# Decode kernel: shared weight loads in folds and PV, PV's blocks picked and p summed on VectorE

## The chip, the core and the metric

The kernel runs on one core of one Trainium2 chip. The metric is device time in microseconds of one execution; three executions of the kernel before took 203.09, 203.16 and 203.21 us (median 203.16). A core has a matrix engine (TensorE, PE in the profile; its weight loads are the rows PEld), VectorE (DVE), ScalarE (ACT), GpSimd (POOL) and SyncE (SP), which here only issues DMAs. SBUF is the working memory with 128 partitions; PSUM is where TensorE writes, in 8 banks of 512 fp32 a partition.

## What is computed

One token passes an attention block and a gated MLP, each with a layer norm in front and a residual behind. Everything is bf16 outside of sums. There are 32 heads of 128, a cache of 4096 positions for each, and a model width of 640.

```
q = (layernorm(x) @ wq)                          # 640 -> 32 heads x 128
scores = einsum("bhqd,bhkd->bhqk", q, k) * 128 ** -0.5
p = softmax(scores)                              # over 4096 positions
o = einsum("bhqk,bhkd->bhqd", p, v)
h = x + o.reshape(1, 1, 4096) @ wo               # 4096 -> 640
g, u = layernorm(h) @ w_gate, layernorm(h) @ w_up        # 640 -> 1728
out = h + (gelu(g) * u) @ w_down                 # 1728 -> 640
```

The caches are 2 x 32 x 4096 x 128 bf16, 67 MB; with the weights the kernel reads 84 MB from HBM.

## The kernel before

**Groups and slots.** The 32 heads are taken in 8 groups of 4. A group's K is one DMA of 4 MB, its V another. In SBUF a tile has 128 partitions: partition 32j + r holds 128 consecutive cache rows of the group's head j (the r-th of 32 such stretches). The tiles go through three slots in the order K0 V0 K1 V1 ... K5 V5 K6 K7 V6 V7 (line 170); V7 comes in two halves. SyncE issues each load when the tile that lay in its slot three places earlier has been used up (`consumed`, lines 180 to 191): a K tile by the last of its four products on VectorE (line 274), a V tile by its last product on TensorE (line 310). Behind the caches SyncE issues wo in three pieces, then the MLP's weights. The first of these, w_down's, waits for PV of group 7 (`free[1]`, lines 381 and 388), and everything behind it in SyncE's queue waits with it.

**Scores** (`score_mult`, `score_exp`). Each K tile is handled in four quarters of 32 rows. VectorE multiplies a quarter by q (line 270, 4096 elements a partition). TensorE adds the 128 products of a row down to 16 with eight products by the identity matrix, which accumulate in one PSUM bank: the fold (line 278). VectorE sums the 16 (line 285). ScalarE takes exp in four activations, one for each head's 32 partitions (line 289); they write p into `p_bd`, and their accumulator output writes the sum of p into `RS`. The order on VectorE is product 0, product 1, reduction 0, product 2, reduction 1, and so on.

`p_bd[partition, row, j]` is zero wherever j is not the partition's own head, so that one matrix product keeps the four heads apart.

**PV** (`pv_group`). 32 products of 512 columns: block b takes p of 4 rows (weights of 16 columns: 4 rows x 4 heads) and V of the same 4 rows (512 columns: 4 rows x 128). It writes 16 PSUM partitions from 32(b mod 4) on, so four column tiles of the array work side by side. Of each 16 x 4 blocks of result only those in which the row of the weights is the row of V are wanted. ScalarE copies the bank to `po_sb` (line 311), and four small fp32 products with the pattern `hs` (line 316, the head sum) pick the wanted blocks and add them up over partitions into `ps_a`. TensorE does the head sum of group G - 1 ahead of PV of group G.

**Softmax's denominator and the projection.** `sum_half(t)` adds `RS` over quarters on VectorE (line 326) and over partitions on TensorE (line 327) for the 16 heads of a half; `finish_half(t)` scales the half (`aT`, line 331), spreads it over partitions (line 336) and leaves it in `aP` (line 339). `proj_part` multiplies it by wo (line 345, 160 products of one column). Then come the residual and layer norm (lines 401 and 402), the gate (line 418), up and down products.

**Order and waits.** `Prog` keeps one list for each engine in the order in which the code adds operations; an engine runs its list in that order. An operation waits for the semaphores of its dependencies, except that TensorE does not wait for itself. So where an operation is added decides what stands behind it in its engine's list.

Of the kernel before, what the change touches and what calls it, by code (L numbers as in the profile page):

```python
# [99 lines left out]
def bass_sequential_preLN__gqa_block_cached__glu_gated_geglu__decode_kernel(nc, A_x, A_k_cache, A_v_cache, A_wq, A_wo, B_x, B_w_gate, B_w_up, B_w_down, out):  # L102
    sb = lambda name, shape, dt: nc.alloc_sbuf_tensor(name, shape, dt)
# [7 lines left out]
    RS = sb("RS", [128, H, 4], FP32)  # L111
    RT = sb("RT", [128, H], FP32)
    x_row = sb("x_row", [1, D], BF16)
    out_row = sb("out_row", [1, D], BF16)
# [7 lines left out]
    po_sb = sb("po_sb", [128, 2, 512], FP32)  # L122
    hs_t = sb("hs_t", [128, 4, 16], FP32)
    hs = sb("hs", [128, 4, 28], FP32)
    aT = sb("aT", [16, 2, 128], BF16)
    aP = sb("aP", [128, 2, 16], BF16)
    sel = sb("sel", [16, 8, 128], BF16)
# [18 lines left out]
    bank = [nc.alloc_psum_tensor("bank%d" % i, [128, 512], FP32) for i in range(8)]  # L146
    ps_f = [bank[0], bank[1]]
    ps_g, ps_u = bank[0], bank[1]
    ps_q = [bank[3], bank[7]]
    ps_a = bank[3]  # L150
    ps_d = bank[3][:, 256:416]
    ps_o = [bank[2], bank[4]]
# [27 lines left out]
    def issue(upto):  # L180
        while state["next"] < min(upto, len(order)):
# [8 lines left out]
                         for i in range(parts)]  # L190
# [18 lines left out]
    GP(lambda e: e.memset(hs[:, :, :], 0.0))  # L209
    c_hs = GP(lambda e: e.affine_select(hs_t[:, :, :], ones_f[:, 0:64].rearrange("p (a b) -> p a b", a=4),  # L210
                                        pattern=[[-32, 4], [-1, 16]], compare_op=ALU.is_equal,
                                        fill=0.0, base=0, channel_multiplier=1), c_ones)
    c_sel2 = GP(lambda e: e.affine_select(sel2[:, :, :], ones_b[0:64, 0:128].rearrange("p (a b) -> p a b", a=64),
                                          pattern=[[1, 64], [0, 2]], compare_op=ALU.is_equal,
# [5 lines left out]
    c_rs = GP(lambda e: e.memset(RS[:, :, :], 0.0))  # L220

    c_po = [V(lambda e, b=b: e.memset(bank[b][:, :], 0.0)) for b in (2, 4)]
    c_hs = V(lambda e: e.reduce_sum(hs[:, :, 12:16], hs_t[:, :, :].rearrange("p t (g j) -> p g j t", g=4), axis=AX.X), c_hs)
# [37 lines left out]
    qc = A(lambda e: e.copy(qb[:, 4:8, :].rearrange("p g d -> p (g d)"), ps_q[1][:, :]), qd)  # L261


    folds, reds, exps, pvs, evs, hds = {}, {}, {}, {}, {}, {}

    def score_mult(s):
        G, n = s // 4, pos[("K", s // 4)]
        kt = view(n)
        u = s % 4
        m = V(lambda e: e.tensor_tensor(  # L270
            out=prod[:, s % 4, :, :], in0=kt[:, 32 * u:32 * u + 32, :],
            in1=qb[:, G, :].unsqueeze(1).to_broadcast([128, 32, DH]), op=ALU.mult),
            landed[n][0], qa, qc, folds.get(s - 4))
        consumed[n] = m

        def fold(e):
            for b in range(8):
                i = e.matmul(ps_f[s % 2][:, :], id_b[:, :], prod[:, s % 4, :, 16 * b:16 * b + 16],  # L278
                             start=(b == 0), stop=(b == 7))
            return i  # L280
        folds[s] = T(fold, m, c_idb, reds.get(s - 2))

    def score_exp(s):
        G = s // 4
        reds[s] = V(lambda e: e.reduce_sum(  # L285
            sc[:, s % 4, :], ps_f[s % 2][:, :].rearrange("p (g d) -> p g d", d=16), axis=AX.X),
            folds[s], exps.get(s - 4))
        for j in range(4):
            x = A(lambda e, j=j: e.activation(  # L289
                p_bd[32 * j:32 * j + 32, G % 2, 32 * (s % 4):32 * (s % 4) + 32, j],  # L290
                sc[32 * j:32 * j + 32, s % 4, :], ACTF.Exp,
                bias=zero_t[32 * j:32 * j + 32, 0:1], scale=INV_SQRT_DH,
                accum_out=RS[32 * j:32 * j + 32, 4 * G + j, s % 4:s % 4 + 1]),
                reds[s], pvs.get(G - 2), c_pbd, c_rs, c_eps)
        exps[s] = x


    def pv_group(G):
        n = pos[("V", G)]
        vt = view(n)  # L300
        po = ps_o[G % 2]
        parts = len(landed[n])
        for k in range(parts):
            def pv(e, k=k):
                for b in range(32 // parts * k, 32 // parts * (k + 1)):
                    a = 32 * (b % 4)
                    i = e.matmul(po[a:a + 16, :], p_bd[:, G % 2, 4 * b:4 * b + 4, :].rearrange("p g j -> p (g j)"),  # L307
                                 vt[:, 4 * b:4 * b + 4, :], start=(b < 4), stop=(b >= 28))
                return i
            pvs[G] = consumed[n] = T(pv, exps[4 * G + 3], landed[n][k], evs.get(G - 2), *c_po)  # L310
        evs[G] = A(lambda e: e.copy(po_sb[:, G % 2, :], po[:, :]), pvs[G], hds.get(G - 2))  # L311

        def head_sum(e):
            g = G % 4
            for r in range(4):
                i = e.matmul(ps_a[0:16, 128 * (G // 4):128 * (G // 4) + 128], hs[:, r, 12 - 4 * g:28 - 4 * g],  # L316
                             po_sb[:, G % 2, 128 * r:128 * r + 128], start=(g == 0 and r == 0), stop=(g == 3 and r == 3))
            return i
        return head_sum


    zs = {}

    def sum_half(t):
        hh = slice(16 * t, 16 * t + 16)
        r = V(lambda e: e.reduce_sum(RT[:, hh], RS[:, hh, :], axis=AX.X), exps[16 * t + 15])
        z = T(lambda e: e.matmul(ps_z[0:16, 0:1], RT[:, hh], ones_f[:, 0:1], start=True, stop=True), r)
        zs[t] = V(lambda e: e.reciprocal(rz[:, t:t + 1], ps_z[0:16, 0:1]), z)

    def finish_half(t):  # L330
        z4 = V(lambda e: e.tensor_scalar(aT[:, t, :], ps_a[0:16, 128 * t:128 * t + 128], rz[:, t:t + 1], None, ALU.mult),
               zs[t], hds[4 * t + 3])

        def spread(e):
            for q in range(8):
                i = e.matmul(ps_z[:, 32:48], sel[:, q, :], aT[:, t, 16 * q:16 * q + 16], start=(q == 0), stop=(q == 7))
            return i
        z5 = T(spread, z4, c_sel)
        return V(lambda e: e.tensor_copy(aP[:, t, :], ps_z[:, 32:48]), z5)
# [61 lines left out]
    h = V(lambda e: e.tensor_add(hT[:, 0:5], xx[:, 0:5], ps_p[:, 0:5]), pr)  # L401
# [91 lines left out]
```

## Time and profile before

| | |
|---|---|
| median of three executions | 203.16 us |
| profiled execution | 203.49 us |
| its span (first to last instruction) | 202.2 us |
| HBM read | 84.23 MB, 417 GB/s over the span |
| TensorE busy, share of the span | 121.6 us, 60% (weight loads 57.9 us, 29%) |
| VectorE busy | 101.2 us, 50% |
| ScalarE busy | 61.0 us, 30% |
| records on TensorE (products + loads), on ScalarE | 1010 + 1010, 273 |
| granted TensorE clock, mean | 0.865 |

The span is from the first to the last instruction of the profiled execution; what an execution takes beyond it lies before and after. Products on TensorE are pipelined and the ends shown are modelled. The profile's 40 slices are 5.06 us each. A line of a timeline or of the list of instruction groups names the source line, the engine, the operation, the tile written and the tile read; in the list of groups the two numbers behind the bar are the busy time in us and the mean duration of one in ns, and behind the second bar stands how long the engine had been idle just before, and who ended that. In the timelines the first two numbers are the start and the length in us.

### The profile page before, as it was taken

Reading aid. Unit: us, or ns where it says so; the run is one execution under the profiler, and the core shown is the slowest. Engines: PE = TensorE matmul, PEld = TensorE weight load, DVE = VectorE, ACT = ScalarE, POOL = GpSimd, SP = SyncE. Lnnn points to the kernel's source line nnn. Section 1 sums busy time; section 2 is a strip of 40 time slices with the busy share of each in tenths; the row PEclk is TensorE's granted clock in tenths of the full one; section 3 lists DMA queues with packets and bytes.
Section 4 is the critical chain, followed back from the end, with each engine's and each line's share of the span. In section 5 each row is a group of like instructions: output and inputs, shape, how many; then the busy total and the mean of one; then the engine's idle time right before and its main releaser. Section 6 shows DMA issues by size and latency. Waiting matters only on the chain.

```text
span 202.2 us, 2506 instructions
## 1 busy us (share of the span) xinstructions
PE 121.6 (60%) x1010; PEld 57.9 (29%) x1010; DVE 101.2 (50%) x106; ACT 61.0 (30%) x273; POOL 5.0 (2%) x14
## 2 busy tenths in 40 slices
PE   0108057566670786395477841976376697788395
PEld 0103023112230223031242310322122234487383
DVE  3200188519912793479259616771877885010221
ACT  2100104621561066105613630355036246300101
POOL 7200000000000000000000000000000000000000
PEclk9999999969999589969879997599799679995555
DMA  9999999999999999999999999999999999999992
GB/s 332 438 410 441 441 421 415 421 463 434 429 421 421 428 447 437 434 421 421 423 441 441 431 421 428 428 436 447 431 421 421 415 421 441 427 396 440 407 407 91
DMA packets 4335, 84.39 MB, mean 417 GB/s; under 512 B 482, under 2 KB 868, under 8 KB 1508
## 3 DMA queue, kind: packets, MB, share of 16 engines
q1 hardware_dynamic: 4322, 84.23, 97.7%
q8 instruction: 8, 0.13, 0.3%
q14 instruction: 3, 0.02, 0.0%
q10 hardware_dynamic: 2, 0.00, 0.0%
HBM read 84.23 MB, written 0.00 MB: 417 GB/s over the span
## 4 chain that ended last, share of the span: by engine, by line
DMA 53%; PE 20%; DVE 19%; ACT 3%; issue 3%; SPq 2%
DMA slot<-in_A_k_cache_dram 44%; DVE prod L270 16%; PE bank L278 13%; DMA slot<-in_B_w_down_dram 9%; PE bank L307 5%; DVE sc L285 3%; ACT p_bd L289 2%; SPq L51 2%; PE bank L316 1%; PE bank L444 0%; DVE out_row L457 0%; ACT po_sb L311 0%
## 5 line engine op out<-in xcount | busy, mean ns | idle before, releaser
L278 PE MATMUL bank<-prod,id_b 128*128 128x512 bf16 x256 | 72.9, 441 | 46.8 <-DVE prod L270 46.7
L270 DVE TENSOR_TENSOR prod<-slot,qb 128x4096 bf16<-128x4096 bf16 x32 | 72.4, 2284 | 34.9 <-DMA slot<-in_A_k_cache_dram 34.9
L289 ACT ACTIVATE p_bd<-sc,zero_t 32x32 bf16<-32x32 f32 x128 | 46.3, 362 | 79.9 <-DVE sc L285 78.7
L278 PEld LDWEIGHTS bank<-prod,id_b 128*128 128x128 bf16 x256 | 26.1, 110 | 94.5 <-DVE prod L270 60.5
L285 DVE TENSOR_REDUCE sc<-bank 128x32 f32<-128x512 f32 x32 | 22.0, 687 | 19.7 <-PE bank L278 19.7
L289 ACT ACTIVATION_READ_ACCUMULATOR p_bd<-sc,zero_t 32x1 f32 x128 | 23.5, 184 | 0.0
L307 PE MATMUL bank<-slot,p_bd 128*16 128x512 bf16 x256 | 18.4, 420 | 7.7 <-ACT p_bd L289 7.7
L307 PEld LDWEIGHTS bank<-slot,p_bd 128*16 128x16 bf16 x256 | 8.3, 95 | 14.6 <-ACT p_bd L289 9.1
L311 ACT COPY po_sb<-bank 128x512 f32<-128x512 f32 x8 | 4.7, 585 | 19.2 <-PE bank L307 19.2
L316 PE MATMUL bank<-po_sb,hs 128*16 128x128 f32 x64 | 9.2, 292 | 1.2 <-ACT po_sb L311 1.2
L256 PE MATMUL bank<-arena,xlnB 128*32 128x512 bf16 x40 | 4.5, 631 | 7.2 <-DMA arena<-in_A_wq_dram 7.2
L414 PE MATMUL bank<-hlnT,slot 128*128 128x1 bf16 (+1 forms) x140 | 6.7, 176 | 3.3 <-DMA slot<-in_B_w_gate_dram 3.3
L414 PEld LDWEIGHTS bank<-hlnT,slot 128*128 128x128 bf16 (+1 forms) x140 | 6.3, 118 | 4.2 <-issue 3.9
L316 PEld LDWEIGHTS bank<-po_sb,hs 128*16 128x16 f32 x64 | 5.9, 102 | 4.8 <-issue 2.1
L345 PE MATMUL bank<-aP,arena 128*128 128x1 bf16 x160 | 6.7, 178 | 0.3 <-DMA arena<-in_A_wo_dram 0.3
L345 PEld LDWEIGHTS bank<-aP,arena 128*128 128x128 bf16 x160 | 6.6, 131 | 0.4 <-issue 0.3
L260 DVE CAST qb<-bank 128x512 bf16<-128x512 f32 x1 | 0.7, 691 | 10.1 <-PE bank L256 10.1
L241 ACT ACTIVATE ln<-ln,eps_t 128x1 f32<-128x1 f32 x2 | 0.6, 294 | 16.8 <-DVE ln L239 16.8
L230 PE MATMUL bank<-one_bf,x_row 1*128 1x1 bf16 x5 | 0.4, 177 | 7.1 <-DMA x_row<-in_A_x_dram 7.1
L256 PEld LDWEIGHTS bank<-arena,xlnB 128*32 128x32 bf16 x40 | 1.6, 141 | 9.2 <-issue 9.2
L261 ACT CAST qb<-bank 128x512 bf16<-128x512 f32 x1 | 0.6, 585 | 10.6 <-PE bank L256 10.6
L401 DVE TENSOR_TENSOR hT<-xx,bank 128x5 f32<-128x5 f32 x1 | 0.2, 161 | 6.6 <-PE bank L345 6.6
(65 smaller groups left out, 26.4 us busy)
## 6 DMA issues: line engine op xcount, KB each, us to landing
slot<-in_A_k_cache_dram SPq DMA_DIRECT2D x8, 4096.0 KB, 21.7
slot<-in_A_v_cache_dram SPq DMA_DIRECT2D x7, 4096.0 KB, 19.3
arena<-in_A_wq_dram SPq DMA_DIRECT2D x1, 5120.0 KB, 15.5
slot<-in_A_v_cache_dram SPq DMA_DIRECT2D x2, 2048.0 KB, 15.2
arena<-in_A_wo_dram SPq DMA_DIRECT2D x1, 2560.0 KB, 23.1
slot<-in_B_w_gate_dram SPq DMA_DIRECT2D x1, 2160.0 KB, 12.8
arena<-in_A_wo_dram SPq DMA_DIRECT2D x1, 1920.0 KB, 27.2
slot<-in_B_w_up_dram SPq DMA_DIRECT2D x1, 1296.0 KB, 14.6
```

The source lines that it names most:

```text
L51: ev = self.op(eng, lambda e: e.dma_start(out, in_), *deps, dma=True)
L256: i = e.matmul(ps_q[hf][32 * j:32 * j + 32, :], xlnB[:, c, :], wq_j[:, c, j, 4 * hf:4 * hf + 4, :], start=(c == 0), stop=(c == 4))
L260: qa = V(lambda e: e.tensor_copy(qb[:, 0:4, :].rearrange("p g d -> p (g d)"), ps_q[0][:, :]), qd)
L270: m = V(lambda e: e.tensor_tensor(out=prod[:, s % 4, :, :], in0=kt[:, 32 * u:32 * u + 32, :], in1=qb[:, G, :].unsqueeze(1).to_broadcast([1 ...
L278: i = e.matmul(ps_f[s % 2][:, :], id_b[:, :], prod[:, s % 4, :, 16 * b:16 * b + 16], start=(b == 0), stop=(b == 7))
L285: reds[s] = V(lambda e: e.reduce_sum(sc[:, s % 4, :], ps_f[s % 2][:, :].rearrange("p (g d) -> p g d", d=16), axis=AX.X), folds[s], exps.ge ...
L289: x = A(lambda e, j=j: e.activation(p_bd[32 * j:32 * j + 32, G % 2, 32 * (s % 4):32 * (s % 4) + 32, j], sc[32 * j:32 * j + 32, s % 4, :], ...
L307: i = e.matmul(po[a:a + 16, :], p_bd[:, G % 2, 4 * b:4 * b + 4, :].rearrange("p g j -> p (g j)"), vt[:, 4 * b:4 * b + 4, :], start=(b < 4) ...
L311: evs[G] = A(lambda e: e.copy(po_sb[:, G % 2, :], po[:, :]), pvs[G], hds.get(G - 2))
L316: i = e.matmul(ps_a[0:16, 128 * (G // 4):128 * (G // 4) + 128], hs[:, r, 12 - 4 * g:28 - 4 * g], po_sb[:, G % 2, 128 * r:128 * r + 128], s ...
L345: r = e.matmul(ps_p[:, c:c + 1], wo_sb[:, t, i, c::5], aP[:, t, i:i + 1], start=(t == 0 and c == 0 and i == 0), stop=(t == 1 and i == 15), ...
L414: i = e.matmul(ps[0:128 if m < 13 else 64, m:m + 1], ws, hlnT[:, c:c + 1], start=(c == 0 and m == 0), stop=(c == 4), skip_group_check=True)
```

## The change

**Folds.** The identity matrix is loaded once for each fold; the seven further products are built by the new `matmul_again`, which emits a product without a weight load in front of it.

**PV.** The weights of a product are now 32 columns (8 rows x 4 heads). Each of 16 such weights is held for two products, one for each half of the 8 rows of V. Four weights, one for each column tile, are loaded with the first half's products; the second half's products follow without loads. The result takes two neighbouring banks, `po`, shared by all groups; before, two single banks alternated.

**Picking blocks.** In place of the copy on ScalarE, VectorE multiplies the two banks by the pattern `m8`, which keeps one of 8 blocks for each partition (`po_m`, 1024 fp32), and sums over the 8 blocks into `po_r`. That sum reads `po_m` with 128 elements, or 512 bytes, between the elements of one sum. PV of the next group waits for the multiplication (`mks`), because the banks are shared. The head sum becomes one product of 128 columns.

**Sums of p.** The activations have no accumulator output any more. VectorE sums `p_bd` over the 128 rows for each of 4 heads (`RT`, read with 4 elements between neighbours) after the group's last exp; this operation is in front of the multiplication by `m8` in VectorE's list. `RS` and its sum are gone.

**Moves.** `sum_half(0)` runs at group 4, `sum_half(1)` after the last PV; the last head sum and `finish_half(1)` come after the first half of the projection. The patterns `hs` and `m8` are made at the start; two PSUM clears go.

```diff
+def matmul_again(nc, out, lhsT, rhs, start, stop, tile, at):
+    e = nc.tensor
+    return e.add_instruction(mybir.InstMatmult(
+        name=nc.get_next_instruction_name(), engine=e.engine, start_tensor_calc=start, stop_tensor_calc=stop,
+        tile_size=tile, tile_position=at, ldweights=False,
+        ins=[e.lower_ap(rhs), e.lower_ap(lhsT)], outs=[e.lower_ap(out)]))
...
         def fold(e):
             for b in range(8):
-                i = e.matmul(ps_f[s % 2][:, :], id_b[:, :], prod[:, s % 4, :, 16 * b:16 * b + 16],
-                             start=(b == 0), stop=(b == 7))
+                args = (ps_f[s % 2][:, :], id_b[:, :], prod[:, s % 4, :, 16 * b:16 * b + 16])
+                if b == 0:
+                    i = e.matmul(*args, start=True, stop=False)
+                else:
+                    i = matmul_again(nc, *args, False, b == 7, (128, 128), (0, 0))
             return i
...
-                bias=zero_t[32 * j:32 * j + 32, 0:1], scale=INV_SQRT_DH,
-                accum_out=RS[32 * j:32 * j + 32, 4 * G + j, s % 4:s % 4 + 1]),
-                reds[s], pvs.get(G - 2), c_pbd, c_rs, c_eps)
+                bias=zero_t[32 * j:32 * j + 32, 0:1], scale=INV_SQRT_DH),
+                reds[s], pvs.get(G - 2), sums.get(G - 2), c_pbd, c_eps)
...
+        sums[G] = V(lambda e: e.reduce_sum(RT[:, 4 * G:4 * G + 4], p_bd[:, G % 2, :, :].rearrange("p g j -> p j g"), axis=AX.X),
+                    exps[4 * G + 3])
+
+        def pv_mm(e, c, half, load):
+            a = 32 * (c % 4)
+            args = (po[a:a + 32, 512 * half:512 * half + 512],
+                    p_bd[:, G % 2, 8 * c:8 * c + 8, :].rearrange("p g j -> p (g j)"),
+                    vt[:, 8 * c + 4 * half:8 * c + 4 * half + 4, :])
+            if load:
+                return e.matmul(*args, start=(c < 4), stop=(c >= 12))
+            return matmul_again(nc, *args, c < 4, c >= 12, (128, 32), (0, a))
+
         for k in range(parts):
             def pv(e, k=k):
-                for b in range(32 // parts * k, 32 // parts * (k + 1)):
-                    a = 32 * (b % 4)
-                    i = e.matmul(po[a:a + 16, :], p_bd[:, G % 2, 4 * b:4 * b + 4, :].rearrange("p g j -> p (g j)"),
-                                 vt[:, 4 * b:4 * b + 4, :], start=(b < 4), stop=(b >= 28))
+                for c4 in range(4 // parts * k, 4 // parts * (k + 1)):
+                    for half in range(2):
+                        for c in range(4 * c4, 4 * c4 + 4):
+                            i = pv_mm(e, c, half, half == 0)
                 return i
-            pvs[G] = consumed[n] = T(pv, exps[4 * G + 3], landed[n][k], evs.get(G - 2), *c_po)
-        evs[G] = A(lambda e: e.copy(po_sb[:, G % 2, :], po[:, :]), pvs[G], hds.get(G - 2))
+            pvs[G] = consumed[n] = T(pv, exps[4 * G + 3], landed[n][k], mks.get(G - 1))
+        mks[G] = V(lambda e: e.tensor_tensor(
+            out=po_m[:, :, :], in0=po[:, :].rearrange("p (b d) -> p b d", b=8),
+            in1=m8[:, :].unsqueeze(2).to_broadcast([128, 8, DH]), op=ALU.mult), pvs[G], c_m8)
+        evs[G] = V(lambda e: e.reduce_sum(po_r[:, G % 2, :], po_m[:, :, :].rearrange("p b d -> p d b"), axis=AX.X),
+                   mks[G], hds.get(G - 2))
 
         def head_sum(e):
             g = G % 4
-            for r in range(4):
-                i = e.matmul(ps_a[0:16, 128 * (G // 4):128 * (G // 4) + 128], hs[:, r, 12 - 4 * g:28 - 4 * g],
-                             po_sb[:, G % 2, 128 * r:128 * r + 128], start=(g == 0 and r == 0), stop=(g == 3 and r == 3))
-            return i
+            return e.matmul(ps_a[0:16, 128 * (G // 4):128 * (G // 4) + 128], hs[:, 12 - 4 * g:28 - 4 * g],
+                            po_r[:, G % 2, :], start=(g == 0), stop=(g == 3))
...
-        r = V(lambda e: e.reduce_sum(RT[:, hh], RS[:, hh, :], axis=AX.X), exps[16 * t + 15])
-        z = T(lambda e: e.matmul(ps_z[0:16, 0:1], RT[:, hh], ones_f[:, 0:1], start=True, stop=True), r)
+        z = T(lambda e: e.matmul(ps_z[0:16, 0:1], RT[:, hh], ones_f[:, 0:1], start=True, stop=True), sums[4 * t + 3])
...
-        if G in (3, NG - 1):
-            sum_half(G // 4)
         if heads is not None:
             hds[G - 1] = T(heads, evs[G - 1], c_hs, qa, qc)
         if G == 4:
+            sum_half(0)
             a0 = finish_half(0)
         heads = pv_group(G)
         issue(pos[("V", G)] + 1 + NSLOT)
-    hds[NG - 1] = T(heads, evs[NG - 1])
-    a1 = finish_half(1)
+    sum_half(1)
...
     proj_part(0, 0, 16, a0, d_wo["0"])
+    hds[NG - 1] = T(heads, evs[NG - 1])
+    a1 = finish_half(1)
     proj_part(1, 0, 12, a1, d_wo["1a"])
     pr = proj_part(1, 12, 16, d_wo["1b"])
```

More of the change, by code (lines that the diff above doesn't have):

```diff
@@ L110, in bass_sequential_preLN__gqa_block_cached__glu_gated_geglu__decode_kernel @@
     p_bd = sb("p_bd", [128, 2, 128, 4], BF16)
-    RS = sb("RS", [128, H, 4], FP32)
     RT = sb("RT", [128, H], FP32)
@@ L121, in bass_sequential_preLN__gqa_block_cached__glu_gated_geglu__decode_kernel @@
     rz = sb("rz", [16, 2], FP32)
-    po_sb = sb("po_sb", [128, 2, 512], FP32)
-    hs_t = sb("hs_t", [128, 4, 16], FP32)
-    hs = sb("hs", [128, 4, 28], FP32)
+    po_m = sb("po_m", [128, 8, DH], FP32)
+    po_r = sb("po_r", [128, 2, DH], FP32)
+    m8_t = sb("m8_t", [128, 8, 4, 4], FP32)
+    m8 = sb("m8", [128, 8], FP32)
+    hs_t = sb("hs_t", [128, 4, 32], FP32)
+    hs = sb("hs", [128, 28], FP32)
     aT = sb("aT", [16, 2, 128], BF16)
@@ L145, in bass_sequential_preLN__gqa_block_cached__glu_gated_geglu__decode_kernel @@
     zero_t = sb("zero_t", [128, 1], FP32)
-    bank = [nc.alloc_psum_tensor("bank%d" % i, [128, 512], FP32) for i in range(8)]
+    psum = lambda i, n=1: nc.alloc_psum_tensor("bank%d" % i, [128, 512 * n], FP32)
+    bank = {0: psum(0), 1: psum(1)}
+    po = psum(2, 2)
+    bank.update({i: psum(i) for i in range(4, 8)})
     ps_f = [bank[0], bank[1]]
     ps_g, ps_u = bank[0], bank[1]
[L149 to L152, printed above, removed]
+    ps_q = [bank[4], bank[7]]
+    ps_a = bank[4]
+    ps_d = bank[4][:, 256:416]
     ps_s = bank[5]
@@ L208, in bass_sequential_preLN__gqa_block_cached__glu_gated_geglu__decode_kernel @@
                                          fill=0.0, base=0, channel_multiplier=-8), c_onesb)
-    GP(lambda e: e.memset(hs[:, :, :], 0.0))
-    c_hs = GP(lambda e: e.affine_select(hs_t[:, :, :], ones_f[:, 0:64].rearrange("p (a b) -> p a b", a=4),
-                                        pattern=[[-32, 4], [-1, 16]], compare_op=ALU.is_equal,
+    c_hz = GP(lambda e: e.memset(hs[:, :], 0.0))
+    c_hs = GP(lambda e: e.affine_select(hs_t[:, :, :], ones_f[:, :].rearrange("p (a b) -> p a b", a=4),
+                                        pattern=[[-1, 4], [-4, 32]], compare_op=ALU.is_equal,
+                                        fill=0.0, base=0, channel_multiplier=1), c_ones)
+    c_m8 = GP(lambda e: e.affine_select(m8_t[:, :, :, :], ones_f[:, :].rearrange("p (a b c) -> p a b c", a=8, b=4),
+                                        pattern=[[-4, 8], [-32, 4], [-1, 4]], compare_op=ALU.is_equal,
                                         fill=0.0, base=0, channel_multiplier=1), c_ones)
@@ L219, in bass_sequential_preLN__gqa_block_cached__glu_gated_geglu__decode_kernel @@
     c_pbd = GP(lambda e: e.memset(p_bd[:, :, :, :], 0.0))
-    c_rs = GP(lambda e: e.memset(RS[:, :, :], 0.0))
-    c_po = [V(lambda e, b=b: e.memset(bank[b][:, :], 0.0)) for b in (2, 4)]
-    c_hs = V(lambda e: e.reduce_sum(hs[:, :, 12:16], hs_t[:, :, :].rearrange("p t (g j) -> p g j t", g=4), axis=AX.X), c_hs)
+    c_hs = V(lambda e: e.reduce_sum(hs[:, 12:16], hs_t[:, :, :], axis=AX.X), c_hs, c_hz)
+    c_m8 = V(lambda e: e.reduce_sum(m8[:, :], m8_t[:, :, :, :].rearrange("p a b c -> p a (b c)"), axis=AX.X), c_m8)
     V(lambda e: e.reduce_sum(par[:, :], par_t[:, :, :], axis=AX.X), c_par)
@@ L261, in bass_sequential_preLN__gqa_block_cached__glu_gated_geglu__decode_kernel @@
     qc = A(lambda e: e.copy(qb[:, 4:8, :].rearrange("p g d -> p (g d)"), ps_q[1][:, :]), qd)
-    folds, reds, exps, pvs, evs, hds = {}, {}, {}, {}, {}, {}
+    folds, reds, exps, sums, pvs, evs, hds = {}, {}, {}, {}, {}, {}, {}
     def score_mult(s):
@@ L300, in pv_group @@
         vt = view(n)
-        po = ps_o[G % 2]
         parts = len(landed[n])
+        sums[G] = V(lambda e: e.reduce_sum(RT[:, 4 * G:4 * G + 4], p_bd[:, G % 2, :, :].rearrange("p g j -> p j g"), axis=AX.X),
[8 more added lines that the diff above has]
+            return matmul_again(nc, *args, c < 4, c >= 12, (128, 32), (0, a))
@@ L319, in pv_group @@
         return head_sum
+    mks = {}
     zs = {}
```

## The prediction

> **What bounds the kernel now.** I read the page's slices and queues first, then the chain of waits, then the timelines of VectorE, TensorE and SyncE for one cache group and for the tail.
>
> ```profile
> DMA  9999999999999999999999999999999999999992
> ...
> q1 hardware_dynamic: 4322, 84.23, 97.7%
> q8 instruction: 8, 0.13, 0.3%
> ```
>
> The DMA engines are busy in every slice but the last, so the time is the length of one unbroken stream of 84.23 MB: what computes is free as long as the queue never runs dry and the work behind the last landings is not longer than it is.
>
> How much room is there in a group? Group 5 on VectorE and TensorE:
>
> ```profile
> 123.06 4.49 DVE L270 TENSOR_TENSOR prod<-slot,qb 128x4096 bf16<-128x4096 bf16 x2 [5.71 <-DMA slot<-in_A_k_cache_dram]
> ...
> 136.72 0.69 DVE L285 TENSOR_REDUCE sc<-bank 128x32 f32<-128x512 f32 x1 [1.39 <-PE bank L278]
> 139.18 1.90 PE L307 MATMUL bank<-slot,p_bd 128*16 128x512 bf16 x32 [1.52 <-ACT p_bd L289]
> 142.50 4.49 DVE L270 TENSOR_TENSOR prod<-slot,qb 128x4096 bf16<-128x4096 bf16 x2 [5.09 <-DMA slot<-in_A_k_cache_dram]
> ```
>
> VectorE starts when K5 lands, is done at 137.4, then idles 5.1 us until K6 lands. From its start to the end of PV it is 141.08 - 123.06 = 18.0 us; K tiles of groups 0 to 6 are started every (142.50 - 25.22)/6 = 19.55 us. In the kernel before, PV's end holds nothing on VectorE. The tail:
>
> ```profile
> 176.39 0.80 SPq L51 DMA_DIRECT2D slot<-in_B_w_down_dram  x2
> 185.90 0.16 DVE L401 TENSOR_TENSOR hT<-xx,bank 128x5 f32<-128x5 f32 x1 [6.60 <-PE bank L345]
> 190.20 3.34 PE L414 MATMUL bank<-hlnT,slot 128*128 128x1 bf16 x70 [3.29 <-DMA slot<-in_B_w_gate_dram]
> 199.62 0.70 PE L444 MATMUL bank<-slot,hm 128*1 128x160 bf16 x16 [0.18 <-DMA slot<-in_B_w_down_dram]
> ```
>
> PV7 ends at 176.37 and frees the slot for the MLP weights (176.39). From hT (185.90) to the gate's input is 2.5 us, so the gate product could start at 188.4 and waits for its weights until 190.2: 1.8 us of room. From there to the end TensorE is nearly full; the last wait is 0.18 us. So lateness of PV7's end is free at first, and then counts one for one.
>
> **The change, part by part.** *Folds.* 224 of 256 weight loads go (L278, 110 ns each), but the loads lie beside the products: eight products take 1.90 us, which is 7 steps of 0.216 and the 0.38 of the last one; a slow-clock fold has the same form at 0.427. I take 0; exposed loads would have made it a gain of at most 8 x 0.11 = 0.9 a fold.
>
> *PV.* 32 products of 512 columns stay; 128 of 256 loads go, the rest get 32 columns for 16. It took 1.90 for 32, again the pace of the products with four column tiles at once. I take 1.90; if a load can't slip under a held weight, four rounds of loads stand free: 4 x (0.095 + a product's latency of 0.05 or so), an estimate of +0.6 from the L307 rows (95 ns a load). The other end, all 32 loads having been exposed, is excluded by the 1.90.
>
> *Exps.* 128 accumulator reads (L289, 184 ns) and 8 copies L311 (585 ns) leave ScalarE. From the first exp of the last quarter to PV is 1.73 us (137.45 to 139.18), four steps of 0.42. Without the read the next activation can start 0.22 after the one before (as the read does now): 3 x 0.22 + 0.36 = 1.03, so 0.7 less before each PV. If activations don't overlap it is 4 x 0.36 = 1.45, 0.3 less.
>
> *VectorE gets three operations a group, in its order behind the last reduction of scores and before the next group's products.* RT over 512 bf16: by L285 (512 elements, 687 ns) 0.69; it runs under PV's 1.90, so nothing. If PV gave no cover it would cost its 0.69. Then the mask (1024 fp32 from PSUM) waits for PV's end, and the sum (po_r) for the mask. Both stand free: VectorE waits for PV now, and what is queued behind them is the next group's products, on which folds, exps and the release of the K slot wait.
>
> ```profile
> L285 DVE TENSOR_REDUCE sc<-bank 128x32 f32<-128x512 f32 x32 | 22.0, 687 | 19.7 <-PE bank L278 19.7
> ...
> L404 DVE TENSOR_TENSOR hX<-id_f,hT 128x640 f32<-128x640 f32 x1 | 0.8, 816 | 0.0
> ...
> L326 DVE TENSOR_REDUCE RT<-RS 128x16 f32<-128x64 f32 x2 | 0.4, 220 | 3.5 <-ACT p_bd L289 3.5
> ...
> L223 DVE TENSOR_REDUCE hs<-hs_t 128x16 f32<-128x64 f32 x1 | 0.3, 257 | 1.3 <-POOL hs_t L210 1.3
> ```
>
> An fp32 operation costs 1.04 ns an element and 0.15 us: 512 give 687, 640 give 816. The mask is 1024 x 1.04 + 0.15 = 1.22. The sum reads po_m with a step of 512 bytes between elements. The only such read in the trace is L223 (step 64 bytes); the same 64 elements in a row (L326) take 37 ns less, which is 0.58 ns an element. Three prices: no penalty (the 37 ns is a fixed cost) 1.22 to 1.26; the row's, 0.15 + 1024 x 1.62 = 1.82; half rate, 0.15 + 1024 x 2.08 = 2.28. I take 1.82, the price of the one row with a like read.
>
> [...]
>
> *Head sums* fall from 8 TensorE records to 2 a group (1.05 to about 0.3 us); they lie in the shadow of exps except for group 6, where they stand before PV7, and group 7.
>
> **The sum.** A group: 18.0 - 0.7 + 1.22 + 1.82 + 0.05 of handoffs = 20.4, against 19.55 of arrivals: VectorE falls 0.85 behind in each of groups 0 to 5, 5.1 in all, and starts K6 at 147.6. (Groups 1 and 4 took 16.5 before, with folds at full clock; the longer pause of TensorE before each group, 3.1 + 2.3 us, should leave all of them cold, since pauses of 3.7 us and more did so before.) The K slots stay ahead of the queue: V6 needs K5's slot by 139.4 (1.0 us before the first ring finishes K6, at 140.4 by its semaphore increment); it is freed at 134.7 + 4.3. From K6's start to the last fold was 170.16 - 142.50 = 27.7, so 175.3; head sum 0.3, PV6 1.9: 177.5. In place of the 0.59 copy come mask and sum, 3.1: 180.6; head sum 0.3, PV7 1.9: 182.8, against 176.4. The MLP weights are issued then; the slowest ring has queued work to 184.7, and the first packet comes 1.0 us after an issue (seen at the start), so the stream may pause 1 to 2 us, hidden as the next lines show. Behind PV7 the order is now the first half of the projection (80 pairs of 42 ns, 3.4), under which mask and sum of group 7 (3.1) vanish; then head sum, aT, spread, aP with handoffs 1.6; second half 3.4: hT at 182.8 + 8.4 = 191.2; gate 2.5 later at 193.7, 3.5 after the 190.2 of before. Less the 0.18 at the end, the span grows by 3.3, to 205.5. The profiled execution took 203.49 for a span of 202.2; the median without a profile is 203.16, and 203.16 + 3.3 = 206.5.
>
> **Rivals.** *A, the cover holds (not slower).* With the sum at 1.22 a group takes 19.8, K6 starts 1.5 late, PV7 ends at 178.6 and the gate is ready at 189.5, before its weights: 203.1. It decides where the sum stays under about 1.32 us; above, each 0.1 costs 0.7 (six groups and PV6). For it: L223 is a single row and its surplus may be fixed. Should late quarters start at full clock, up to 1.5 us of fold time come back as well.
>
> *B, shorter programs speed the stream.* TensorE loses 448 of 2020 records, ScalarE 136 of 273. The DMA records show 8 fetches of 16 KB for TensorE of 1.0 to 1.1 us, and by each transfer's 16 semaphore increments one ring falls about 1.5 us further behind at each; at the end the last ring is 2.3 behind the first, and a ring without a fetch at most 1.4. Without the fetch at 186.1 the last would be 0.3 better, without all 0.9: 202.3 to 202.9, say 202.6, and only with A. [...]
>
> *C, half rate.* At 2.28 the mechanism is the forecast's: PV7 ends at 186.0, the gate starts at 196.9, 209.7.
>
> *D, held weights cost PV time.* +0.6 in each of eight PVs with a cheap sum: 178.6 + 4.8 = 183.4, gate 194.3, 207.1. Against it: the 1.90 has no gap for loads today.
>
> **Numbers.** Forecast 0.42, A 0.30, B 0.08, C 0.12, D 0.08. The range of the forecast alone is 204.3 to 208.1 (sum 1.5 to 2.05). 202.6 to 210.0 takes in A, most of B, D and C. A change of under 0.2% (0.4 us) can't be told from none: faster is B and 0.06 of A, 0.14; same 0.19 of A and 0.01, 0.20; slower the rest, 0.66.
>
> **What would show it.** Right: po_r at 1.8 us each, VectorE's wait for K tiles gone in groups 1 to 6, PV7 ending near 183, the gate's wait for its weights gone, and more than one slice without DMA at the end. Wrong: po_r near 1.25 and the gate still waiting for DMA (A); fetches fewer and the last landing before 199.3 (B); PV groups well over 1.9 (D); folds shorter than 1.9 at full clock would say the loads were not hidden.

## The result and the profile after

| | before | after |
|---|---|---|
| median | 203.13 us (4 executions) | 214.47 us (213.22 to 216.63, 4 executions) |
| ratio, 95% interval | | 1.0537 (1.0492 to 1.0582) |
| profiled execution, its span | 203.49, 202.2 us | 214.57, 213.2 us |
| granted TensorE clock, mean | 0.865 | 0.794 |
| TensorE busy; weight loads | 121.6; 57.9 us | 121.6; 27.4 us |
| VectorE busy; ScalarE busy | 101.2; 61.0 us | 129.7; 50.3 us |

The kernel is 5.4% slower. (Ratios leave out executions more than 1.5% above the fastest of their kernel, here the one of 216.63 us; medians and ranges hold them all.) The direction and the path of the loss are the forecast's, its size is over three times as large: 11.3 us for 3.3.

The slices of after (the clock granted to TensorE, DMA share) and its data queue:

```profile
PEclk9999679785995599758995895599667979996555
DMA  9899999999999999999599989997999499989992
q1 hardware_dynamic: 4322, 84.23, 93.9%
```

The stream is broken: slices at 5, 7 and 4 tenths (209, 270, 138 GB/s) stand between full ones, and the queue is busy for 93.9% in place of 97.7%. The instruction queue q8 has 6 fetches for 8, which bought nothing that shows. The clock row of before reads

```profile
PEclk9999999969999589969879997599799679995555
```

so in the cache groups fewer slices are at 9 in after: over groups 0 to 5 the mean is 0.79 for 0.90.

Group 5 of after, VectorE, TensorE and ScalarE in order of time; it answers to the group shown of before (each line: start, length, engine, line, operation, tiles):

```profile
133.31 4.48 DVE L284 TENSOR_TENSOR prod<-slot,qb 128x4096 bf16<-128x4096 bf16 x2
136.05 3.15 PE L28 MATMUL bank<-prod,id_b 128*128 128x512 bf16 x7
146.92 0.69 DVE L302 TENSOR_REDUCE sc<-bank 128x32 f32<-128x512 f32 x1 [1.40 <-PE bank L28]
147.65 1.48 ACT L306 ACTIVATE p_bd<-sc,zero_t 32x32 bf16<-32x32 f32 x4 [0.60 <-DVE sc L302]
149.16 0.69 DVE L318 TENSOR_REDUCE RT<-p_bd 128x4 f32<-128x512 bf16 x1 [1.55 <-ACT p_bd L306]
149.19 0.58 PE L327 MATMUL bank<-slot,p_bd 128*32 128x512 bf16 x4 [1.98 <-ACT p_bd L306]
...
152.10 0.65 PE L28 MATMUL bank<-slot,p_bd 128*32 128x512 bf16 x4
152.79 1.23 DVE L338 TENSOR_TENSOR po_m<-bank,m 128x1024 f32<-128x1024 f32 x1 [2.94 <-PE bank L28]
154.05 1.87 DVE L341 TENSOR_REDUCE po_r<-po_m 128x128 f32<-128x1024 f32 x1
155.84 2.28 DVE L284 TENSOR_TENSOR prod<-slot,qb 128x4096 bf16<-128x4096 bf16 x1
```

Behind K0 no product of K waits for a DMA any more: K6's begins (155.84) as the sum of `po_m` ends. PV, which took 1.90 in the group shown of before, goes from 149.19 to 152.75: each pass of four column tiles takes 0.43 where 0.216 is full clock. Between the starts of K0 and K6 lie 155.84 - 24.78 = 131.06 us, 21.84 a group. The groups of instructions (busy time, mean ns; idle before):

```profile
L284 DVE TENSOR_TENSOR prod<-slot,qb 128x4096 bf16<-128x4096 bf16 x32 | 72.3, 2281 | 4.4 <-DMA slot<-in_A_k_cache_dram 4.4
L338 DVE TENSOR_TENSOR po_m<-bank,m 128x1024 f32<-128x1024 f32 x8 | 9.8, 1224 | 16.1 <-PE bank L28 14.5 <-PE bank L356 1.6
L341 DVE TENSOR_REDUCE po_r<-po_m 128x128 f32<-128x1024 f32 x8 | 15.2, 1897 | 0.3
```

VectorE's wait for K tiles fell from 34.9 to 4.4 us (the one at K0). In the mean the mask takes 1.22, the sum 1.90 and the sum of p (L318) 0.68. The tail:

```profile
190.48 0.80 SPq L59 DMA_DIRECT2D slot<-in_B_w_down_dram  x2
201.54 3.36 PE L443 MATMUL bank<-hlnT,slot 128*128 128x1 bf16 x70 [1.50 <-DVE hlnT L431]
```

PV7 ends at 190.44 and frees the slot; the gate starts at 201.54, and it waits for `hlnT`, no longer for its weights.

### The profile page after: what moved, and what is told of

Its sections match the earlier page's. It is cut to its first block, busy times and chain, and to the rows that moved or that the text cites. A ratio compares the mean times of both kernels' runs of the same rounds, so it can differ in the third digit from the quotient of the medians.

```text
span 213.2 us, 1929 instructions
## 1 busy us (share of the span) xinstructions
PE 121.6 (57%) x962; PEld 27.4 (13%) x610; DVE 129.7 (61%) x127; ACT 50.3 (24%) x137; POOL 5.5 (3%) x14
## 3 DMA queue, kind: packets, MB, share of 16 engines
q1 hardware_dynamic: 4322, 84.23, 93.9%
## 4 chain that ended last, share of the span: by engine, by line
DVE 44%; PE 37%; DMA 11%; ACT 4%; issue 3%; SPq 0%; DVEq 0%
DVE prod L284 25%; PE bank L28 21%; DMA slot<-in_A_k_cache_dram 11%; DVE po_r L341 7%; DVE sc L302 7%; PE bank L327 5%; DVE po_m L338 5%; PE bank L294 4%; ACT p_bd L306 3%; PE bank L443 3%; PE bank L374 2%; PE bank L473 1%; PE bank L346 1%; PE bank L452 0%; DVE out_row L486 0%
## 5 line engine op out<-in xcount | busy, mean ns | idle before, releaser
L28 PE MATMUL bank<-prod,id_b 128*128 128x512 bf16 x224 | 67.0, 449 | 0.0
L294 PE MATMUL bank<-prod,id_b 128*128 128x512 bf16 x32 | 15.2, 476 | 57.2 <-DVE prod L284 57.2
L327 PE MATMUL bank<-slot,p_bd 128*32 128x512 bf16 x128 | 16.4, 484 | 10.9 <-ACT p_bd L306 10.9
L338 DVE TENSOR_TENSOR po_m<-bank,m 128x1024 f32<-128x1024 f32 x8 | 9.8, 1224 | 16.1 <-PE bank L28 14.5
L294 PEld LDWEIGHTS bank<-prod,id_b 128*128 128x128 bf16 x32 | 3.5, 110 | 124.0 <-DVE prod L284 124.0
L28 PE MATMUL bank<-slot,p_bd 128*32 128x512 bf16 x128 | 16.9, 497 | 0.0
L341 DVE TENSOR_REDUCE po_r<-po_m 128x128 f32<-128x1024 f32 x8 | 15.2, 1897 | 0.3
L318 DVE TENSOR_REDUCE RT<-p_bd 128x4 f32<-128x512 bf16 x8 | 5.5, 684 | 8.2 <-ACT p_bd L306 8.2
L327 PEld LDWEIGHTS bank<-slot,p_bd 128*32 128x32 bf16 x128 | 4.6, 111 | 22.4 <-ACT p_bd L306 14.0
L346 PE MATMUL bank<-po_r,hs 128*16 128x128 f32 x16 | 3.4, 294 | 3.4 <-DVE po_r L341 3.2
L275 ACT CAST qb<-bank 128x512 bf16<-128x512 f32 x1 | 0.6, 586 | 10.3 <-PE bank L270 10.3
```

Of the source, the lines that this page charges most:

```text
L28: return e.add_instruction(mybir.InstMatmult(name=nc.get_next_instruction_name(), engine=e.engine, start_tensor_calc=start, stop_tensor_ca ...
L294: i = e.matmul(*args, start=True, stop=False)
L318: sums[G] = V(lambda e: e.reduce_sum(RT[:, 4 * G:4 * G + 4], p_bd[:, G % 2, :, :].rearrange("p g j -> p j g"), axis=AX.X), exps[4 * G + 3])
L327: return e.matmul(*args, start=(c < 4), stop=(c >= 12))
L338: mks[G] = V(lambda e: e.tensor_tensor(out=po_m[:, :, :], in0=po[:, :].rearrange("p (b d) -> p b d", b=8), in1=m8[:, :].unsqueeze(2).to_br ...
L341: evs[G] = V(lambda e: e.reduce_sum(po_r[:, G % 2, :], po_m[:, :, :].rearrange("p b d -> p d b"), axis=AX.X), mks[G], hds.get(G - 2))
```

## The experiments

### Does VectorE's place behind PV make the loss?

**e_vec: the kernel before with two idle operations.** The edit, on arrays that nothing else uses:

```diff
+        dmk = V(lambda e: e.tensor_tensor(out=dm[:, :, :], in0=dz[:, :, :], in1=dz[:, :, :], op=ALU.mult), pvs[G], c_dz)
+        V(lambda e: e.reduce_sum(dr[:, :], dm[:, :, :].rearrange("p b d -> p d b"), axis=AX.X), dmk)
         evs[G] = A(lambda e: e.copy(po_sb[:, G % 2, :], po[:, :]), pvs[G], hds.get(G - 2))
```

> The kernel before, unchanged, with two VectorE operations more behind each PV and in front of the next group's products: a product over 1024 fp32 and a sum that reads its result 512 bytes apart, on arrays of their own that nothing else uses (the first waits for PV, the second for the first). Theory: VectorE's turn behind PV alone makes the loss, and TensorE's pause under it takes its clock to half in PV. A group goes from 18.0 us to 18.0 + 1.22 + 1.87 + 0.05 = 21.1 at the clock of before, and to 22 or so with PV at half clock in most groups; K6 starts at 152 to 158, granted clock about 0.80, and the time is 212 to 217. Rival: the loss needs the rest of the change too (one pair of banks for all PVs, fewer loads, the later head sum); then the clock stays near 0.86, PV at 1.90, K6 at 152 and the time at 206 to 210.

Measured: 217.45 us (216.72 to 218.3), ratio 1.0707 (1.0683 to 1.073). Its timeline behind PV of group 4:

```profile
127.28 1.90 PE L311 MATMUL bank<-slot,p_bd 128*16 128x512 bf16 x32 [0.73 <-ACT p_bd L293]
...
129.23 1.23 DVE L315 TENSOR_TENSOR dm<-dz 128x1024 f32<-128x1024 f32 x1 [2.47 <-PE bank L311]
130.49 1.87 DVE L316 TENSOR_REDUCE dr<-dm 128x128 f32<-128x1024 f32 x1
132.28 4.48 DVE L274 TENSOR_TENSOR prod<-slot,qb 128x4096 bf16<-128x4096 bf16 x2
```

PV, the two operations and the next K tile stand in one row. K6 starts at 153.33, as the theory had it (152 to 158), and the granted clock is 0.818. So 3.1 us of VectorE behind PV are enough for a loss as large as the change's, with none of its other parts. In two points the theory missed: the time lies just above its 212 to 217, and four of the six PVs here took 1.90. A group is 21.4 us all the same, near the 21.1 worked out without half clock, and K6 is 10.8 us later than in the kernel before; in after it is 13.3 later. The rest of e_vec's loss is in the tail, which keeps the order of before and is longer than after's: PV7 ends at 192.4 for 190.4, and 24.6 us follow for 22.8. So the time lies above after's.

**e_defer: the same operations, later in VectorE's order.** The mask and the sum of groups 0 to 5 are added behind the second product of the next K tile:

```diff
+            if i == 1 and late:
+                late.pop()()
...
+        if G < NG - 2:
+            late.append(pick)
+        else:
+            pick()
```

> The changed kernel with one move: for groups 0 to 5 the multiplication by m8 and the sum po_r are placed behind the second product of the next group's K tile in VectorE's list, not in front of the first. Nothing is removed. Theory (the two operations, 1.22 + 1.9 us, stand behind PV's end and in front of the next group, so a group takes 21.8 us on VectorE where K tiles could come every 19.5): VectorE is free for the next group after RT, about 17 to 18 us from its start, the two operations fill the 1.5 us in which it waits for the first fold and delay the rest by some 1.6, and the stream of DMAs is never dry: 203.0 to 205.0, VectorE waiting for K tiles again. Rival (held weights or shorter TensorE programs slow TensorE, or the shared PSUM banks do): the work is all still there, so 211 or more.

Measured: 205.23 us (203.28 to 206.45), ratio 1.007 (1.0037 to 1.0104). Group 4's start in its timeline:

```profile
103.20 4.49 DVE L284 TENSOR_TENSOR prod<-slot,qb 128x4096 bf16<-128x4096 bf16 x2 [0.75 <-DMA slot<-in_A_k_cache_dram]
105.77 1.67 PE L28 MATMUL bank<-prod,id_b 128*128 128x512 bf16 x7
107.61 1.22 DVE L339 TENSOR_TENSOR po_m<-bank,m 128x1024 f32<-128x1024 f32 x1
108.86 1.93 DVE L342 TENSOR_REDUCE po_r<-po_m 128x128 f32<-128x1024 f32 x1
```

VectorE waits for K tiles again (10.7 us in all), since the 3.1 us now lie beside fold and exp of the new tile. The same work in another place costs 2.1 us in place of 11.3. The profiled execution (203.48) is one of four near 203.4; the other six took 205.2 to 206.5.

**e_defer_tail: group 6's head sum behind PV7 as well.** The edit stands on top of e_defer's; besides, the mask now names the sum of the group before as a dependency, which VectorE's order gives anyway.

```diff
-        if heads is not None:
+        if heads is not None and G < NG - 1:
             hds[G - 1] = T(heads, evs[G - 1], c_hs, qa, qc)
+        last = heads
...
+    hds[NG - 2] = T(last, evs[NG - 2])
     sum_half(1)
```

> As e_defer (205.2, in its profile PV7 started behind PV6, mask, sum, head sum, one after the other), and the head sum of group 6 is issued behind PV7, so that PV7 waits only for group 6's mask and no longer for its sum. Theory: what e_defer still lost lay in this chain; PV7 ends 1.9 + 0.4 us earlier, the gate's input is ready 2 us before its weights in nearly all executions, and the time is that of the data stream, 202.6 to 203.4, less scattered than e_defer's 203.3 to 206.5. Rival: the masks and sums inside the groups still empty the queue now and then; then the time stays at 204.5 to 205.5.

Measured: 203.10 us (202.95 to 203.4), ratio 1.0001 (0.9993 to 1.001). From its timeline, the issue that PV7 releases, and the gate:

```profile
176.59 0.80 SPq L59 DMA_DIRECT2D slot<-in_B_w_down_dram  x2
189.74 3.34 PE L452 MATMUL bank<-hlnT,slot 128*128 128x1 bf16 x70 [2.78 <-DMA slot<-in_B_w_gate_dram]
```

The gate waits for its weights again. PV7 ends at 176.56, in e_defer's profile at 179.67: it starts 1.6 us earlier and takes 1.91 for 3.45, in which a pass came every 0.43 us, the pace of half clock again. What e_defer still lost was the chain PV6, mask, sum, head sum, PV7.

**e_actpick and e_actpick_early: the picking off VectorE.** ScalarE copies both banks, and eight head-sum products pick the blocks; `matmul_again`, the plain exps and the sum of p stay.

```diff
-        mks[G] = V(lambda e: e.tensor_tensor(
...
+        mks[G] = evs[G] = A(lambda e: e.copy(po_m[:, G % 2, :, :].rearrange("p b d -> p (b d)"), po[:, :]), pvs[G], hds.get(G - 2))
...
+            for b in range(8):
+                i = e.matmul(ps_a[0:16, 128 * (G // 4):128 * (G // 4) + 128], hs[:, b, 12 - 4 * g:28 - 4 * g],
+                             po_m[:, G % 2, b, :], start=(g == 0 and b == 0), stop=(g == 3 and b == 7))
```

> The changed kernel with its shared loads, its exps without accumulator output and its sum of p on VectorE, but the picking of blocks goes back to ScalarE and TensorE: ScalarE copies both banks, and the head sum is eight products of 128 columns, one for each block. Nothing stands behind PV on VectorE. Theory: only VectorE's turn behind PV cost time. A group takes 18.0 - 0.2 again, VectorE waits for K tiles (30 us and more in all), clock about 0.86, and the time is 202.6 to 203.4. Rival: something else of the change costs too (the shared banks, the sum of p, the moved head sum); then 204 or more.

Measured: 204.63 us (204.17 to 205.08), ratio 1.0074 (1.0061 to 1.0086): 1.2 above what was expected. VectorE waits for K tiles again, though for 23.6 us and not for 30; the stream is unbroken, and the rest is in the tail:

```profile
181.07 3.53 PE L336 MATMUL bank<-po_m,hs 128*16 128x128 f32 x16
191.64 3.38 PE L434 MATMUL bank<-hlnT,slot 128*128 128x1 bf16 x70 [1.50 <-DVE hlnT L422]
```

Group 7's head sum stands behind the first half of the projection, and its 16 records take 3.53 us, while those of group 3 took 1.92. That is 1.84 times as long, about as at half clock; in before the granted clock is 0.5 from 181.71 us to the end. The next kernel moves that one line ahead of the projection:

```diff
+    hds[NG - 1] = T(heads, evs[NG - 1])
     proj_part(0, 0, 16, a0, d_wo["0"])
-    hds[NG - 1] = T(heads, evs[NG - 1])
```

> e_actpick with group 7's head sum ahead of the first half of the projection. In e_actpick it stood behind, at half clock: 16 records in 3.53 us, and the gate started at 191.6 in place of 190.2. Theory: that alone made its 204.6; ahead of the projection the head sum takes 1.9, the gate's input is ready at 189.3 or earlier, before its weights, and the time is 202.9 to 203.4. Rival: another part of the change costs the rest; then 204 or more.

Measured: 203.34 us (203.04 to 204.12), ratio 1.0014 (1.0 to 1.0029). The head sum takes 1.92 there:

```profile
179.40 1.92 PE L336 MATMUL bank<-po_m,hs 128*16 128x128 f32 x16 [1.09 <-ACT po_m L331]
```

Six of the ten executions took 203.0 to 203.4, the other four, the profiled one among them, 203.9 to 204.1. So the shared loads, the shared banks, the exps without accumulators and the sum of p cost 0.2 to 0.3 us together (0 to 0.6 by the interval); the loss is the picking on VectorE.

### What made the group 1.4 us longer than forecast?

**e_warm: TensorE kept busy.** Products of 512 columns on constants, into an idle bank (`busy(e, n)` issues n of them), six ahead of each PV but the last, twenty behind PVs 0 to 5, and ten behind PV6 and, which the expectation doesn't say, PV7:

```diff
+        if G < NG - 1:
+            T(lambda e: busy(e, 6))
...
+        T(lambda e: busy(e, 20 if G < NG - 2 else 10))
```

> The changed kernel with products on constants added on TensorE where it pauses: 6 of 512 columns ahead of each PV, 20 behind PV of groups 0 to 5, 10 behind PV 6; they go to a PSUM bank that nobody reads. Theory: of the 2.3 us by which a group is longer than K tiles come, most is half clock: first folds 1.5 us longer, PV 2.9 instead of 1.9 us. With the clock kept up a group takes 21.8 - 1.5 - 1.0 = 19.3 and the time falls to 203.5 to 207. If the clock plays no part, 214 or more, since TensorE has more to do.

Measured: 204.20 us (204.17 to 204.41), ratio 1.0054 (1.0039 to 1.0069). A group of its timeline, from the product of K4 to that of K5:

```profile
104.38 4.48 DVE L289 TENSOR_TENSOR prod<-slot,qb 128x4096 bf16<-128x4096 bf16 x2
106.94 1.67 PE L28 MATMUL bank<-prod,id_b 128*128 128x512 bf16 x7
...
120.83 4.49 PE L282 MATMUL bank<-ones_b,id_b 128*128 128x512 bf16 x20
120.94 1.23 DVE L344 TENSOR_TENSOR po_m<-bank,m 128x1024 f32<-128x1024 f32 x1 [1.07 <-PE bank L28]
124.03 2.28 DVE L289 TENSOR_TENSOR prod<-slot,qb 128x4096 bf16<-128x4096 bf16 x1
```

Mask and sum are where they were and as long as they were, PV is 1.91 and the first fold at full clock (granted, from K0's start to K6's: 0.97 in the mean, for 0.79 in after). From K1's start to K6's it is (143.41 - 46.25)/5 = 19.43 a group against 21.84, and VectorE waits for no K tile behind K0: half clock was worth 2.4 us a group, about what the group is longer than the arrivals (21.84 for 19.55). The ten products behind PV7 hold the projection back from 178.40 to 180.73, and the gate, at 191.46, waits for its input; that is probably the 1.1 us by which the time stays above before's.

**e_warm_pv: the clock of PV alone.** Of e_warm only the six products ahead of PV.

```diff
+        if G < NG - 1:
+            T(lambda e: busy(e, 6))
         if heads is not None:
             hds[G - 1] = T(heads, evs[G - 1], c_hs, qa, qc)
```

> The changed kernel with the constant products only ahead of PV (six a group, under the wait for the last exps), none behind it: the clock is to be full in PV, and folds stay as they were (the first of each group at half clock). Theory: of 2.5 us a group that half clock costs, 1.0 are PV's. PV is 1.91 in groups 0 to 5 in place of 2.91, a group takes 20.9, K6 starts at 25 + 6 x 20.9 = 150.4, and the time is 214.5 - 6 = 208.5, within 1. Rival: half clock only moves elsewhere (PV at full clock is paid back in later folds), as the whole changed kernel with full-clock PVs in some groups took the same 214.5 with its loads restored; then the group stays at 21.4 or more and the time at 211 or more.

Measured: 210.92 us (210.18 to 211.62), ratio 1.0383 (1.0356 to 1.0411). Group 2's PV ends, mask, next K tile:

```profile
84.03 0.39 PE L332 MATMUL bank<-slot,p_bd 128*32 128x512 bf16 x4
...
84.67 1.23 DVE L343 TENSOR_TENSOR po_m<-bank,m 128x1024 f32<-128x1024 f32 x1 [1.28 <-PE bank L28]
87.72 4.48 DVE L289 TENSOR_TENSOR prod<-slot,qb 128x4096 bf16<-128x4096 bf16 x2
```

All six PVs take 1.91 to 1.92; a group is (150.22 - 25.05)/6 = 20.86, and K6 starts at 150.22 (expected 150.4). For the groups that is the theory's number to 0.05 us, and not the rival's 21.4. The time is 2.4 us over the theory's and close to the rival's 211, so only a part of the gain at K6 reaches the end. In the profile (210.18, the fastest of the four) K6 is 5.6 us earlier than in after, and the gate 4.7: from K6 to PV6 it is 28.0 us for 27.1. The folds there are not longer; the experiment's own six products stand between the last fold (its end is 177.01) and PV6 (178.25), where after's PV6 follows its last fold at once. Why the other three executions are up to 1.4 us slower stays open; two of them had a lower mean clock (0.83, 0.849 for 0.87).

**e_loads: the loads restored.** All products of folds and PV load their weights again, the rest is after's.

```diff
-                    i = matmul_again(nc, *args, False, b == 7, (128, 128), (0, 0))
+                    i = e.matmul(*args, start=False, stop=(b == 7))
...
-            return matmul_again(nc, *args, c < 4, c >= 12, (128, 32), (0, a))
+            return e.matmul(*args, start=(c < 4), stop=(c >= 12))
```

> The changed kernel with a weight load again in front of every product of folds and PV; all else as changed. Theory: loads lie beside the products, so 213 to 216 as the changed kernel. Rival (without loads the products of folds and PV run slower, or TensorE is granted less clock because it is less busy): the 10 us come back in good part, 203 to 209, with a granted clock nearer to 0.86 than to 0.79.

Measured: 214.51 us (213.23 to 214.8), ratio 1.0548 (1.0514 to 1.0581), the same as after. Its PV of group 4:

```profile
126.28 0.65 PE L327 MATMUL bank<-slot,p_bd 128*32 128x512 bf16 x4
```

Half clock there too. The six PVs took 1.91 three times, then 2.59, 3.60 and 2.35: the lengths at full and at half clock (1.91, 3.60) are after's with held weights (1.91, 3.56), so held weights neither lengthen PV nor shorten it. With fewer PVs at half clock K6 starts 2.3 us earlier than in after (153.51); PV7 then took 3.57 for 2.01, and the end is the same.

### The strided sum, and the fetches

**e_contig, and once more as e_contig_again.** `po_m` is laid out so that the sum reads neighbours and the mask writes 32 bytes apart.

```diff
-    po_m = sb("po_m", [128, 8, DH], FP32)
+    po_m = sb("po_m", [128, DH, 8], FP32)
...
-            out=po_m[:, :, :], in0=
+            out=po_m[:, :, :].rearrange("p d b -> p b d"), in0=
...
-po_m[:, :, :].rearrange("p b d -> p d b"), axis=AX.X
+po_m[:, :, :], axis=AX.X
```

> The changed kernel with po_m kept the other way round (8 blocks of one column side by side), so that the sum po_r reads in a row and the multiplication by m8 writes 32 bytes apart. Theory (the read 512 bytes apart costs 0.65 us a sum): the sum takes 1.22 instead of 1.9; if writing apart is free the group gains 0.65, seven times 0.65 = 4.5 us, 209.0 to 210.5; if the multiplication slows by as much, 214. Rival (the operations' length is not what sets the group): 213 to 216 with a sum of 1.22.

> The same kernel as e_contig, to have the time and a profile once more. Theory: striding costs the same on either side, mask 2.0 and sum 1.22 make 3.2 together, and the time depends on which PVs and folds fall to half clock, so it lies between 210 and 217 and differs between executions by more than 1 us. Rival: a contiguous sum is worth something that the operations' durations do not show; then it is near 211 again with little scatter, with groups of 21.3 us or less.

Measured: 211.22 us at first (ratio 1.0383, 1.0343 to 1.0422), 213.51 the second time (1.0478, 1.042 to 1.0536). The two groups in the second profile:

```profile
L338 DVE TENSOR_TENSOR po_m<-bank,m 128x1024 f32<-128x1024 f32 x8 | 16.1, 2014 | 12.2 <-PE bank L28 9.3 <-PE bank L356 2.9
L341 DVE TENSOR_REDUCE po_r<-po_m 128x128 f32<-128x1024 f32 x8 | 9.8, 1220 | 0.3
```

The sum gains 0.68 and the mask loses 0.79. Together they are 3.23 us, 0.11 more than after's, so the first theory's second case came (the mask slows by as much), though most executions stayed below the 214 it gave. The second profile (211.48) shows why: five of its six PVs took 1.91 and one 2.74, a mean of 2.05 for after's 2.91. A group is 21.07 for 21.84, so 0.77 shorter, where PV alone gives 0.86; what is missing is about the 0.11 of the mask and sum. The clock goes with the time in the other executions too: they took 210.3 and 210.5 at a granted clock of 0.822, 211.5 and 212.9 at 0.814 and 0.815, 211.9 at 0.806, 214.1 at 0.793; after's took 213.2 to 214.6 at 0.791 to 0.794. All this speaks against a gain that the durations don't show. Why fewer PVs fell to half clock here than in after stays open.

**e_folds: the kernel before with shared fold loads alone.** The edit to `fold` is the change's own:

```diff
+                if b == 0:
+                    i = e.matmul(*args, start=True, stop=False)
+                else:
+                    i = matmul_again(nc, *args, False, b == 7, (128, 128), (0, 0))
```

> The kernel before with the shared loads of the folds alone: 224 weight loads fewer, everything else as it was. Theory: the loads lay beside the products, and the data stream sets the end: 203.1, within 0.3. Rival: 224 records fewer spare TensorE one fetch of 16 KB or so, which sits in the data rings: 202.8 or less, with fewer fetches in the profile and a last landing 0.3 earlier.

Measured: 203.09 us, ratio 0.9998 (0.9989 to 1.0006). From its queues:

```profile
q8 instruction: 7, 0.11, 0.2%
```

One fetch fewer, and no gain. e_defer_tail has six fetches for eight, and 203.10.

## Why the prediction was wrong, step by step

**Right: the bound and the mechanism.** The queued operations behind PV used up the 5 us of VectorE's wait, the wait for K tiles went, PV7 was late, the gate waited for its input. Mask (1.22) and sum of p (0.69 under PV's cover) were 1.224 and 0.684. The sum of `po_m` was put at 1.82 from one row and took 1.87 in the groups, 1.90 in the mean, far above the 1.32 below which rival A would have held. Of the signs named, one did not come: the DMA row ends with one low slice, as before, and not with more. Behind K6 the working holds, in part by luck, since PV6 and PV7 ran at full clock here (e_loads' PV7 took 3.57 for 2.01): from K6's start to PV7's end 34.6 for 35.2, PV7 to the gate 11.1 for 10.9, gate to the end of the span 11.7 for 11.8. K6 itself started at 155.84 for 147.6, and this is the whole miss: 8.2 us, 1.4 a group.

**The failed step: "It took 1.90 for 32, again the pace of the products with four column tiles at once. I take 1.90"**, in the sum of the group, 18.0 - 0.7 + 1.22 + 1.82 + 0.05. In after the six PVs took 3.45, 2.50, 3.49, 1.91, 2.56 and 3.56, a mean of 2.91. The forecast saw the clock fall for the first folds ("should leave all of them cold") and didn't carry it to PV, which stands behind a pause of its own. The trace of before had shown it, in group 0:

```profile
41.34 3.22 PE L307 MATMUL bank<-slot,p_bd 128*16 128x512 bf16 x32 [2.49 <-ACT p_bd L289]
```

Group 3's took 3.2 too, and only group 5's 1.90 was used. In before, VectorE's wait of 5 us hid such a PV; with the wait gone it counts in full. e_warm_pv prices it: with PV at full clock K6 starts 5.6 us earlier. The length of the pause alone does not decide it: the one ahead of after's PV of group 5 was 1.98 us long and PV ran at half clock, while the same 1.98 left e_defer's PV of group 3 at full clock (1.91). What picks the groups can be read from the clock in after's trace: its changes lie 3.41 us or a whole multiple of that apart, and the clock of such a step goes with how long TensorE was busy in the step before. Ahead of the PV of group 5 this was 1.43 us (145.86 to 149.27); ahead of the PV of group 3, which took 1.91, it was 2.39 (101.49 to 104.90). The last section has the counts of before and after.

**The other mis-sized term: exps, "so 0.7 less before each PV".** From the first exp of the last quarter to PV it is now 1.54 us (147.65 to 149.19) for 1.73: four activations of 0.362 at 0.37 apart, one after the other. They don't overlap; the other end of that step (1.45) was nearly right. So 0.2 is gained in place of 0.7. That is 0.5 a group, some 3 us by K6. Both terms together: 20.4 + 0.5 + 1.0 = 21.9, measured 21.84; with PV at full clock 20.9, measured 20.86 in e_warm_pv.

**Folds and PV loads at nothing** held: at full clock a fold takes 1.89 in after (142.19 to 144.08) for 1.90 and PV 1.91 for 1.90, e_folds takes the time of before, and e_loads that of after. **Rival D** (+0.6 a PV from held weights; the latency of 0.05 in it was an estimate that no run shows) has the right symptom, a longer PV, and the wrong cause: e_loads has the long PVs with all loads in place, and e_warm_pv has PVs of 1.91 with held weights. **Rival C** (2.28 for the sum) is refuted by 1.90. **Rival B** gains nothing: with one and two fetches fewer and the stream unbroken, the time is that of before within 0.1%. But both runs still have fetches (seven and six), so the 0.3 us that B put on the one at 186.1 was not tested by itself. The range ended at 210.0 because it varied the price of the sum and, in D, of PV's loads; the clock's price was not in it.

## What to carry to other kernels

Moving work to an engine with idle time is free only in the place where that engine idles: the same 3.1 us cost 11 in front of the next tile's products, 2 behind two of them, and nothing once the last chain was loosened too. When a change lengthens the pauses of TensorE, price each of its stages at half clock as well (PV took 3.56 us there for 1.91), looking through all groups of the trace for the slow ones that the old wait has hidden. And this kernel, which waits for its data, gained nothing from shorter programs; the versions that undid the loss ended at 203.1 to 203.3, and none was faster than the kernel before.

## What the runs showed of the hardware

- The clock and an in-order wait feed each other, as group 5 of after has it: mask and sum of group 4 (3.1 us) and the first product of K5 (2.28) leave TensorE idle for 5.42 us; its first fold takes 3.55 us, where 1.89 is full clock, and PV 3.56, where 1.91 is; VectorE waits 2.94 us for that PV, and 1.07 for the PV of 1.91 in e_warm's group 4. Filling TensorE's pauses with useless products made the changed kernel 10.3 us faster (214.47 to 204.20).
- In the traces of before and after, the changes of the granted clock lie 3.41 us or a whole multiple of that apart, and the clock of such a step goes with TensorE's busy share in the step before. From 25 us (in before from its first recorded change, at 31.52) to 170 us, 54 steps are at full clock: all 15 that were busy for 42% or less were followed by half clock, and 38 of the 39 at 46% or more by full clock (the other, at 53%, holds the small products of `sum_half(0)` and `finish_half(0)` in group 4 of after). Of the 28 steps at half clock, all 17 that were busy for 78% or more were followed by full clock, and all 11 at 73% or less by half clock.
- A sum over fp32 that lie 512 bytes apart took 1.87 to 1.90 us for 1024 elements, contiguous 1.22; writing them 32 bytes apart took 2.01 for 1.22. For 1024 elements the stride cost 0.68 us where it was read (1.90 less 1.22, the means) and 0.79 where it was written.
- Without an accumulator read between them, activations of 32 elements follow one another at 0.37 us and last 0.362; the read of before (0.184) began 0.22 after its activation's start, lay mostly beside that activation's end, and cost 0.05 each (0.42 apart).
